# One kernel, several edits: a weight load in two column halves with another front, and a third product buffer with the attention work in three excursions

## The chip, the cores and the metric

The kernel runs on one core of a Trainium2 chip. Its time is the device time of one execution in microseconds; the figure for a kernel is the median of its runs. Beside it there is one profiled execution, whose trace gives every instruction of the five engines (PE for matmuls, with PEld for its weight loads; DVE, ACT and POOL for vector work; SP, which issues transfers) with start and duration, counted from the start of the span.

## The reference

Two branches read the same normalised tokens and are added to the input: local attention with dilation, and a gated MLP that mixes over the sequence.

```python
x  = A_x                              # 1 x 2048 x 512
xn = _layernorm(x)
# attention: 32 heads of 16; token s sees s, s-2, ..., s-14
q, k, v = split(xn @ wqkv)
logits  = einsum('bhsd,bhswd->bhsw', q, k[idx]) * 16 ** -0.5   # idx = s - 2w, masked below 0
a       = einsum('bhsw,bhswd->bhsd', softmax(logits), v[idx]) @ wo
# gated MLP: 512 -> 2 x 688
z  = gelu(xn @ w_in)
z1 = z[..., :688]
z2 = _layernorm(z[..., 688:])
g  = einsum('ts,bsf->btf', w_sp, z2) + b_sp[:, None]
b  = (z1 * g) @ w_out
return x + a + b
```

All inputs and the output are bf16.

## The kernel before

Tokens are cut into 16 tiles of 128 (`NT`), features into 4 chunks of 128 (`C`), and the attention work into two halves of 1024 tokens (`hb`). The order on every engine is written out by hand: each engine runs its instructions in the order in which the lines of the kernel issue them, and a wait holds up all that stands behind it on that engine.

**Front.** SP loads x's first four tiles in three transfers, then `w_z2` (the z2 half of `w_in`, 688 columns) in one (L172), then more of x and `wqk`. PE runs matmuls on ones (`spin`, L98) until data comes. A tile is normalised by statistics (`ln_stats`, L183, DVE), a root (`roots`, ACT), a reciprocal (`recip`, DVE) and `ln_apply` (L188, DVE, writes `xn`), and is turned into `xnT`, which has features on the partitions. Tiles 0 to 3 are transposed on PE (`transpose_pe`, L209) and copied out of PSUM by ACT or DVE. Tiles 4 to 15 go in pairs through the loop at L388: DVE does the statistics and starts a Newton iteration for the inverse root (`ln_newton`, L196), POOL runs its eight steps (L203 to L207), DVE applies it, and SP transposes by DMA (`transpose_dma`, L218).

**Middle, up to L477.** PE computes z2 tiles (`z2_part`, L227: 8 matmuls of 344 columns a tile, then a Gelu on ACT that also sums the row into `zsum`), q and k (`qk_pair` and `qk_chunk`: 8 matmuls of 512 columns, then a cast on ACT into `qk`) and v (`v_pair`, L280). ACT squares each z2 tile for its second moment (`z2_square`, L237); `z2_stats` and `z2_norm` turn sums into mean and inverse root and normalise all 16 tiles on DVE.

For the attention logits DVE multiplies q by shifted k (`products(hb, p)`, L298: two of the eight window positions at a time, 128 x 8192 elements, into a buffer `pr` of a pool of two), and PE sums over the 16 elements of each head with 0/1 weights (`reduce_heads(hb, p)`, L305: 16 matmuls with a 32-column stationary operand). `softmax_top`, `softmax_exp` and `softmax_norm` follow on DVE and ACT. `reduce_heads` and `v_pair` fill PE with matmuls that use 32 of its columns at a time (`tile_position`); the kernel goes into such work and back several times between L438 and L476. Where `prp` has no free buffer, `products` waits on DVE until PE has read one.

**End, from L482.** Sixteen times `mix(j)` (32 matmuls on z2, L492) and `z1_tile(j)`, then the gate; between them DVE works through the attention average (`av_ops`); after the last tile PE computes both output projections (L639, L648) and DVE adds x.

Of the kernel before, what the change touches and what calls it, by code (L numbers as in the profile page):

```python
# [18 lines left out]
H = 32  # L19
DH = 16  # L20
DHA = 14
W = 8
DIL = 2
HALO = 16
# [21 lines left out]
def kernel(  # L46
# [38 lines left out]
    def bank_pair(name, two=False):  # L85
        turn[0] += 1
        pool = ps_b if turn[0] % 3 == 0 and not two else ps_a
        return pool.tile([P, 2, 512], F32, name=name, tag="mm")

    b16 = const.tile([NT, P], BF16, name="b16")  # L90
    A.dma_start(b16[:], B_b_sp.rearrange("(j p) -> j p", p=P))


    ones = const.tile([P, P], BF16, name="ones")
    V.memset(ones[:], 1.0)
# [2 lines left out]
    def spin(n):  # L98
        for _ in range(n):
            PE.matmul(idle[:, 0, 0:P], ones[:], ones[:], start=True, stop=True)  # L100

    spin(26)

    ident = const.tile([P, P], BF16, name="ident")
    G.memset(ident[:], 0.0)
# [4 lines left out]
    for c in range(C):  # L110
# [6 lines left out]
    G.affine_select(out=mask[:], in_=mask[:], compare_op=ALU.is_ge, fill=NEG,  # L117
                    base=-DIL * (W - 1), pattern=[[DIL, W], [1, HALO]], channel_multiplier=0)
    b_col = const.tile([P, NT], F32, name="b_col")
    stats = const.tile([P, NT, 6], F32, name="stats")  # L120
    mv = const.tile([P, NT, 2], F32, name="mv")
    rstd = const.tile([P, NT], F32, name="rstd")
# [3 lines left out]
    V.memset(eps_t[:], EPS)  # L126
    zsum = const.tile([P, NT], F32, name="zsum")
    zsq = const.tile([P, NT], F32, name="zsq")
    zmean = const.tile([P, NT], F32, name="zmean")
    zvar = const.tile([P, NT], F32, name="zvar")  # L130
    zrstd = const.tile([P, NT], F32, name="zrstd")

    z2 = base.tile([P, NT, FH], BF16, name="z2")
# [14 lines left out]

    early = ExitStack()
    e1 = early.enter_context(tc.tile_pool(name="e1", bufs=1))  # L150
    xqp = early.enter_context(tc.tile_pool(name="xqp", bufs=3))
    xnp = early.enter_context(tc.tile_pool(name="xnp", bufs=6))
    w_z2 = e1.tile([P, C, FH], BF16, name="w_z2")
    wqk = e1.tile([P, C, 2, D], BF16, name="wqk")
    junk = e1.tile([P, FH], BF16, name="junk")


    w_in_r = B_w_in.rearrange("(k p) f -> p k f", p=P)
# [9 lines left out]
    x0 = xqp.tile([P, 4, D], BF16, name="xq")  # L168
    SP.dma_start(x0[:, 0, :], x2[0:P, :])  # L169
    SP.dma_start(x0[:, 1, :], x2[P:2 * P, :])  # L170
    SP.dma_start(x0[:, 2:4, :], x2[2 * P:4 * P, :].rearrange("(i p) d -> p i d", p=P))  # L171
    SP.dma_start(w_z2[:], w_in_r[:, :, FH:F])  # L172
    xq.append(x0)
    load_x(1)
    for s in range(2):
# [7 lines left out]
    def ln_stats(i):  # L183
        xs = xq[i // 4][:, i % 4, :]
        V.bn_stats(stats[:, i, :], xs)
        V.bn_aggr(mv[:, i, :], stats[:, i, :])

    def ln_apply(i):  # L188
        xn = xnp.tile([P, D], BF16, name="xn")
        V.tensor_scalar(xn[:], xq[i // 4][:, i % 4, :], mv[:, i, 0:1], rstd[:, i:i + 1], ALU.subtract, ALU.mult)  # L190
        return xn

    def roots(a, b):
        A.activation(rstd[:, a:b], mv[:, a:b, 1], ACT.Sqrt, bias=eps_t[:])

    def ln_newton(a, b):  # L196

        sl = slice(a, b)
        y, h, t = rstd[:, sl], hv[:, sl], nt[:, sl]
        V.tensor_scalar(h, mv[:, sl, 1], EPS, -0.5 / NEWTON_K, ALU.add, ALU.mult)  # L200
        V.tensor_scalar(t.bitcast(I32), h.bitcast(I32), 1, 0x3FFFFFFF, ALU.logical_shift_right, ALU.bitwise_and)
        V.tensor_scalar(y.bitcast(I32), t.bitcast(I32), -1, SEED, ALU.mult, ALU.add)
        for c in NEWTON_C:  # L203
            G.tensor_tensor(t, y, y, ALU.mult)
            G.tensor_tensor(t, t, h, ALU.mult)
            G.tensor_scalar(t, t, c, None, ALU.add)
            G.tensor_tensor(y, y, t, ALU.mult)  # L207

    def transpose_pe(i, xn):  # L209
        pt = ps_aux.tile([P, C, P], BF16, name="pt", tag="aux")  # L210
        for c in range(C):
            PE.transpose(pt[:, c, :], xn[:, c * P:(c + 1) * P], ident[:])  # L212
        if i < 2:
            A.copy(xnT[:, :, i * P:(i + 1) * P], pt[:])
        else:
            V.tensor_copy(xnT[:, :, i * P:(i + 1) * P], pt[:])

# [3 lines left out]
    def z2_start(i):  # L221
        pz = bank_pair("pzb")
        for kc in range(C):
            z2_part(i, pz, kc)
        return pz

    def z2_part(i, pz, kc):  # L227
        for hh in range(2):
            PE.matmul(pz[:, hh, 0:FHALF], xnT[:, kc, i * P:(i + 1) * P],  # L229
                      w_z2[:, kc, hh * FHALF:(hh + 1) * FHALF],  # L230
                      start=(kc == 0), stop=(kc == C - 1))

    def z2_gelu(i, pz):
        A.activation(z2[:, i, :].rearrange("p (a b) -> p a b", a=2), pz[:, :, 0:FHALF],  # L234
                     ACT.Gelu_apprx_tanh, accum_out=zsum[:, i:i + 1])

    def z2_square(i):  # L237
        A.activation(junk[:], z2[:, i, :], ACT.Square, accum_out=zsq[:, i:i + 1])  # L238

    def z2_tile(i):  # L240
        z2_gelu(i, z2_start(i))

    def z2_stats():
        V.tensor_scalar(zmean[:], zsum[:], 1.0 / FH, None, ALU.mult)
        V.tensor_tensor(zvar[:], zmean[:], zmean[:], ALU.mult)
        V.scalar_tensor_tensor(zvar[:], zsq[:], 1.0 / FH, zvar[:], ALU.mult, ALU.subtract)
        A.activation(zrstd[:], zvar[:], ACT.Sqrt, bias=eps_t[:])

    def z2_norm():
        V.reciprocal(zrstd[:], zrstd[:])  # L250
        for i in range(NT):
            V.tensor_scalar(z2[:, i, :], z2[:, i, :], zmean[:, i:i + 1], zrstd[:, i:i + 1],
                            ALU.subtract, ALU.mult)

    def qk_chunk(b, c):
        tsl = slice(b * 512, (b + 1) * 512)
        pq = bank_pair("pq")
        for s in range(2):
            for kc in range(C):
                PE.matmul(pq[:, s, :], wqk[:, kc, s, c * P:(c + 1) * P], xnT[:, kc, tsl],  # L260
                          start=(kc == 0), stop=(kc == C - 1))
        at = HALO + b % 2 * 512
        A.copy(qk[b // 2][:, :, c, at:at + 512], pq[:])  # L263
# [32 lines left out]
    prs = {}  # L296

    def products(hb, p):  # L298
        pr = prp.tile([P, 2, C, SB], BF16, name="pr")
        off = HALO - DIL * (W - 1 - 2 * p)  # L300
        V.tensor_tensor(pr[:], qk[hb][:, 0, :, HALO:HALO + SB].unsqueeze(1).broadcast_to([P, 2, C, SB]),  # L301
                        shifted(qk[hb][:, 1, :, off:off + SB]), ALU.mult)
        prs[hb, p] = pr
# [43 lines left out]
    def recip(i):  # L347
        V.reciprocal(rstd[:, i:i + 1], rstd[:, i:i + 1])

    pb = ps_aux.tile([P, NT], BF16, name="pb", tag="aux")  # L350
    PE.transpose(pb[:], b16[:], ident[0:NT, 0:NT])
    spin(9)
    ln_stats(0)
    roots(0, 1)
    A.copy(b_col[:], pb[:])
    ln_stats(1)
    roots(1, 2)
    recip(0)
    transpose_pe(0, ln_apply(0))
    recip(1)  # L360
    spin(4)
    transpose_pe(1, ln_apply(1))
    spin(4)
    ln_stats(2)
    roots(2, 3)
    ln_stats(3)
    roots(3, 4)
    pz0 = z2_start(0)
    z2_gelu(0, pz0)
    recip(2)  # L370
    xn2 = ln_apply(2)
    recip(3)
    xn3 = ln_apply(3)
    pz1 = bank_pair("pzb")
    for kc in range(2):
        z2_part(1, pz1, kc)
    transpose_pe(2, xn2)
    for kc in range(2, C):
        z2_part(1, pz1, kc)
    transpose_pe(3, xn3)  # L380
    z2_gelu(1, pz1)
    z2_tile(2)
    z2_tile(3)


# [2 lines left out]
    for g in groups + (None,):  # L388
        if g:
            for i in range(*g):  # L390
                ln_stats(i)
            ln_newton(*g)
        if prev:
            for i in range(*prev):
                transpose_dma(i, ln_apply(i))
            if prev[0] == 6:
                SP.dma_start(wv[:], wqkv_r[:, :, 2 * D:3 * D])
        prev = g


# [14 lines left out]
    qk_chunk(1, 2)  # L415
    z2_square(5)
    qk_chunk(1, 3)
    for j in range(5):
        load_wsp(j)
        if j == 1:  # L420
            SP.dma_start(w_z1[:], w_in_r[:, :, 0:FH])


    V.tensor_copy(qk[1][:, 1, :, 0:HALO], qk[0][:, 1, :, SB:SB + HALO])
    products(0, 0)
    products(0, 1)
    z2_square(6)
    z2_tile(7)
    qk_chunk(2, 0)
    qk_chunk(2, 1)  # L430
    z2_square(7)
    qk_chunk(2, 2)
    qk_chunk(2, 3)
    z2_tile(8)
    qk_chunk(3, 0)
    z2_square(8)
    qk_chunk(3, 1)
    reduce_heads(0, 0)  # L438
    reduce_heads(0, 1)
    products(0, 2)  # L440
    products(0, 3)
    v_pair(0)
    v_pair(1)
    qk_chunk(3, 2)
    z2_tile(9)
    qk_chunk(3, 3)
    z2_square(9)
    z2_tile(10)
    z2_square(10)
    z2_tile(11)  # L450
    reduce_heads(0, 2)
    reduce_heads(0, 3)
    products(1, 0)
    v_pair(2)
    products(1, 1)
    softmax_top(0)
    z2_square(11)
    v_pair(3)
    z2_tile(12)
    z2_square(12)  # L460
    z2_tile(13)
    z2_square(13)
    z2_tile(14)
    z2_square(14)
    z2_tile(15)
    z2_square(15)
    v_pair(4)
    z2_stats()
    z2_norm()
    v_pair(5)  # L470
    reduce_heads(1, 0)
    reduce_heads(1, 1)
    products(1, 2)
    softmax_exp(0)
# [231 lines left out]
```

## Time and profile before

| | |
|---|---|
| median of 3 runs | 206.74 us (206.56 to 206.85) |
| the profiled execution | 206.28 us, span 204.6 us |
| PE busy | 199.7 us, granted clock 1.0 |
| DVE, ACT, POOL busy | 165.9, 93.6, 16.1 us |
| first z2 matmul, first q/k matmul, first mix | 6.73, 11.84, 73.16 us |
| matmuls of L492, L260 + L272, L229, L285, L310 (whole span) | 512, 128, 128, 256, 128 |

In a view of the timeline a row gives the start and the duration in us, the engine, the line, the operation, output and inputs with their shapes, how many instructions are merged in the row, and in brackets the idle time ahead of them and what ended it. In the chain of work a row gives start, duration and what the end of the program depended on at that time. "PEclk" on the page is the granted TensorE clock in tenths.

### The profile page before, as it was taken

What the parts mean: (1) busy time and instruction counts of PE and PEld (TensorE: products, weight loads), DVE (VectorE), ACT (ScalarE), POOL (GpSimd) and SP (SyncE); (2) the same over time, 40 slices, a digit from 0 to 9 for tenths busy, and PEclk for the clock granted to TensorE, in tenths of its full rate; (3) what the DMA queues carried; (4) which work ended last, traced back from release to release, by engine and by line L of the source; (5) the groups of instructions that cost most, each with busy time, mean ns of one, the idle gap of its engine ahead of it and who ended that gap; (6) DMA issues with size and microseconds to landing.
All of it is one profiled execution on the core that took longest, in us unless ns stands there. A gap on an engine that the chain in (4) does not pass through costs nothing.

```text
span 204.6 us, 4062 instructions
## 1 busy us (share of the span) xinstructions
PE 199.7 (98%) x1666; PEld 120.1 (59%) x1666; DVE 165.9 (81%) x192; ACT 93.6 (46%) x145; POOL 16.1 (8%) x82
## 2 busy tenths in 40 slices
PE   7999999999999999999999999999999999999994
PEld 6655544555566666656666666666666664444442
DVE  4799949659299499989999999999999988335263
ACT  3868897676879996335733331223333311000000
POOL 5045640000000000100000000000000000000000
PEclk9999999999999999999999999999999999999999
DMA  6974957999000004707857799999756225015633
GB/s 167 365 225 79 187 107 153 187 215 145 0 3 0 3 0 41 170 20 161 125 119 153 176 201 187 196 165 205 141 144 141 56 48 80 10 41 153 240 109 96
DMA packets 67395, 25.64 MB, mean 125 GB/s; under 512 B 57152, under 2 KB 67248, under 8 KB 67248
## 3 DMA queue, kind: packets, MB, share of 16 engines
q1 hardware_dynamic: 66960, 25.24, 58.2%
q8 instruction: 13, 0.21, 0.5%
q10 hardware_dynamic: 416, 0.14, 0.3%
q14 instruction: 6, 0.05, 0.1%
HBM read 9.79 MB, written 2.10 MB: 58 GB/s over the span
## 4 chain that ended last, share of the span: by engine, by line
PE 95%; DMA 2%; SPq 1%; DVE 0%; issue 0%
PE pg L492 37%; PE pq L260 10%; PE po L639 10%; PE pzb L229 9%; PE pz L504 9%; PE pv L285 7%; PE po L648 6%; PE pl L310 4%; PE pq L272 3%; DMA w_z<-in_B_w_in_dram 2%; PE po L621 1%; PE pt L212 0%; SPq L171 0%; DVE ot L623 0%; SPq L170 0%; SPq L169 0%
## 5 line engine op out<-in xcount | busy, mean ns | idle before, releaser
L492 PE MATMUL pg<-z,wspT 128*128 128x344 bf16 x512 | 77.3, 309 | 0.0
L492 PEld LDWEIGHTS <-wspT 128*128 128x128 bf16 x512 | 50.0, 98 | 24.9 <-issue 0.4
L301 DVE TENSOR_TENSOR pr<-qk 128x8192 bf16<-128x8192 bf16 x8 | 35.0, 4424 | 7.4 <-PE pl L310 7.4
L495 ACT ACTIVATE gs<-pg,b_col 128x688 bf16<-128x688 f32 x16 | 13.4, 835 | 52.8 <-PE pg L492 52.8
L558 DVE TENSOR_TENSOR pw<-vp,a_sb 128x4096 bf16<-128x4096 bf16 x16 | 36.2, 2286 | 0.0
L260 PE MATMUL pq<-xnT,wqk 128*128 128x512 bf16 x96 | 21.5, 379 | 0.0
L504 PE MATMUL pz<-w_z,xnT 128*128 128x344 bf16 x128 | 21.3, 309 | 0.0
L229 PE MATMUL pzb<-w_z,xnT 128*128 128x344 bf16 x128 | 20.1, 309 | 0.3 <-DMA w_z<-in_B_w_in_dram 0.3
L639 PE MATMUL po<-wout,uT 128*128 128x512 bf16 x90 | 19.8, 379 | 0.0
L563 DVE TENSOR_TENSOR pw<-pw 128x4096 bf16<-128x4096 bf16 x8 | 18.3, 2289 | 0.1
L655 DVE TENSOR_TENSOR ot<-po,xr 128x512 bf16<-128x512 f32 x15 | 9.7, 687 | 9.4 <-PE po L648 6.9
L229 PEld LDWEIGHTS <-xnT 128*128 128x128 bf16 x128 | 12.3, 98 | 7.2 <-issue 0.7
L504 PEld LDWEIGHTS <-xnT 128*128 128x128 bf16 x128 | 12.4, 98 | 6.5 <-issue 0.4
L260 PEld LDWEIGHTS <-wqk 128*128 128x128 bf16 x96 | 9.3, 98 | 10.9 <-issue 0.4
L639 PEld LDWEIGHTS <-uT 128*128 128x128 bf16 x90 | 8.7, 98 | 10.7 <-issue 0.4
L263 ACT CAST qk<-pq 128x1024 bf16<-128x1024 f32 x12 | 12.2, 1013 | 5.4 <-PE pq L260 5.4
L285 PE MATMUL pv<-xnT,wv 128*32 128x512 bf16 x256 | 14.6, 380 | 0.0
L509 ACT ACTIVATE z<-pz 128x688 bf16<-128x688 f32 x16 | 11.9, 745 | 5.6 <-PE pz L504 5.2
L238 ACT ACTIVATE junk<-z 128x688 bf16<-128x688 bf16 x16 | 12.5, 779 | 0.2
L234 ACT ACTIVATE z<-pzb 128x688 bf16<-128x688 f32 x16 | 11.8, 737 | 1.4 <-PE pzb L229 1.4
L648 PE MATMUL po<-wo_r,op 32*128 32x512 bf16 x224 | 12.3, 374 | 0.0
L285 PEld LDWEIGHTS <-wv 128*32 128x32 bf16 x256 | 9.4, 139 | 4.6 <-issue 0.3
(81 smaller groups left out, 167.5 us busy)
## 6 DMA issues: line engine op xcount, KB each, us to landing
xr<-in_A_x_dram SPq DMA_DIRECT2D x4, 512.0 KB, 4.2
out_dram<-ot SPq DMA_DIRECT2D x15, 128.0 KB, 1.8
wo_r<-in_A_wo_dram SPq DMA_DIRECT2D x4, 448.0 KB, 5.0
w_z<-in_B_w_in_dram SPq DMA_DIRECT2D x2, 688.0 KB, 4.9
xq<-in_A_x_dram SPq DMA_DIRECT2D x2, 512.0 KB, 7.0
wqk<-in_A_wqkv_dram SPq DMA_DIRECT2D x2, 512.0 KB, 7.1
wout<-in_B_w_out_dram SPq DMA_DIRECT2D x1, 640.0 KB, 5.0
a_sb<-in_A_x_dram SPq DMA_DIRECT2D x1, 512.0 KB, 9.2
```

What stands on the lines that cost most here:

```text
L229: PE.matmul(pz[:, hh, 0:FHALF], xnT[:, kc, i * P:(i + 1) * P], w_z2[:, kc, hh * FHALF:(hh + 1) * FHALF], start=(kc == 0), stop=(kc == C - 1))
L238: A.activation(junk[:], z2[:, i, :], ACT.Square, accum_out=zsq[:, i:i + 1])
L260: PE.matmul(pq[:, s, :], wqk[:, kc, s, c * P:(c + 1) * P], xnT[:, kc, tsl], start=(kc == 0), stop=(kc == C - 1))
L285: PE.matmul(pv[32 * k:32 * k + 32, dd, :].rearrange("p (b t) -> p b t", b=NB), wv_v[:, kc, 2 * d2 + dd, :], xnT_g[:, kc, :, k, :], start=( ...
L301: V.tensor_tensor(pr[:], qk[hb][:, 0, :, HALO:HALO + SB].unsqueeze(1).broadcast_to([P, 2, C, SB]), shifted(qk[hb][:, 1, :, off:off + SB]), ...
L492: PE.matmul(pg[:, hh, 0:FHALF], wsps[j][:, k, :], z2[:, k, hh * FHALF:(hh + 1) * FHALF], start=(k == 0), stop=(k == NT - 1))
L495: A.activation(gs[:], pg[:, :, 0:FHALF], ACT.Identity, bias=b_col[:, j:j + 1])
L504: PE.matmul(pz[:, hh, 0:FHALF], xnT[:, kc, j * P:(j + 1) * P], w_z1[:, kc, hh * FHALF:(hh + 1) * FHALF], start=(kc == 0), stop=(kc == C - 1))
L558: V.tensor_tensor(pw[:], shifted(vp[:, :, hb, off:off + P]), a_sb[:, 2 * p:2 * p + 2, osl].unsqueeze(2).broadcast_to([P, 2, DH, P]), ALU.mult)
L563: V.tensor_tensor(pws[p - 1][:], pws[p - 1][:], pw[:], ALU.add)
L639: PE.matmul(pos[jj, k][:], uT[:, m, i * P:(i + 1) * P], wout[:, m, :], start=first and m == 0, stop=not first and m == MCH - 1)
L648: PE.matmul(pos[jj, k][:], op[32 * k:32 * k + 32, d, jj * P:(jj + 1) * P], wo_r[32 * k:32 * k + 32, d, :], start=first and d == 0, stop=(n ...
```

## The change

Front: `w_z2` is loaded in two halves of 344 columns, the first ahead of x's tiles 2 and 3. The load of `b_sp` at the start and its transpose on PE go; later a DMA transpose and a POOL copy make `b_col`. Tile 1's statistics are made by ACT with two accumulating activations, ahead of and behind the root of tile 0. Evacuations of tiles 0 and 1 are split in two. The z2 matmuls of tiles 0 and 1 are issued by column half. In the loop over pairs `ln_newton(*g)` is issued behind the applies and transposes of the pair before, and runs tile by tile with two-operation steps.

Middle: a third product buffer `prx`, placed where `xq` and `xn` lay, serves every third product; three products and three reductions follow one another; the z2 tiles 9 to 15 stand together; tiles 7, 8, 13, 14 and 15 (`ZV`) get mean and variance from DVE's `bn_stats` instead of sums from ACT.

```diff
+ZV = (7, 8, 13, 14, 15)
-    A.dma_start(b16[:], B_b_sp.rearrange("(j p) -> j p", p=P))
-    spin(26)
+    spin(35)
...
     SP.dma_start(x0[:, 1, :], x2[P:2 * P, :])
+    SP.dma_start(w_z2[:, :, 0:FHALF], w_in_r[:, :, FH:FH + FHALF])
     SP.dma_start(x0[:, 2:4, :], x2[2 * P:4 * P, :].rearrange("(i p) d -> p i d", p=P))
-    SP.dma_start(w_z2[:], w_in_r[:, :, FH:F])
+    SP.dma_start(w_z2[:, :, FHALF:FH], w_in_r[:, :, FH + FHALF:F])
...
     def ln_newton(a, b):
...
-        for c in NEWTON_C:
-            G.tensor_tensor(t, y, y, ALU.mult)
-            G.tensor_tensor(t, t, h, ALU.mult)
-            G.tensor_scalar(t, t, c, None, ALU.add)
-            G.tensor_tensor(y, y, t, ALU.mult)
+        for i in range(a, b):
+            y, h, t = rstd[:, i:i + 1], hv[:, i:i + 1], nt[:, i:i + 1]
+            for c in NEWTON_C:
+                G.tensor_scalar(t, y, y, h, ALU.mult, ALU.mult)
+                G.tensor_scalar(y, t, c, y, ALU.add, ALU.mult)
...
         if i < 2:
-            A.copy(xnT[:, :, i * P:(i + 1) * P], pt[:])
+            for c in range(0, C, 2):
+                A.copy(xnT[:, c:c + 2, i * P:(i + 1) * P], pt[:, c:c + 2, :])
...
+    def z2_half(i, pz, hh):
+        for kc in range(C):
+            z2_part(i, pz, kc, (hh,))
...
+    def z2_moments(i):
+        for hh in range(2):
+            V.bn_stats(zst[:, i, hh, :], z2[:, i, hh * FHALF:(hh + 1) * FHALF])
+        V.bn_aggr(zmv[:, i, :], zst[:, i, :, :])
...
     def products(hb, p):
-        pr = prp.tile([P, 2, C, SB], BF16, name="pr")
+        pr = (prx if (4 * hb + p) % 3 == 2 else prp).tile([P, 2, C, SB], BF16, name="pr")
...
-    pb = ps_aux.tile([P, NT], BF16, name="pb", tag="aux")
-    PE.transpose(pb[:], b16[:], ident[0:NT, 0:NT])
-    spin(9)
+    A.activation(zrstd[:, 0:1], eps_t[:], ACT.Sqrt)
     ln_stats(0)
+    A.activation(junk[:, 0:D], x0[:, 1, :], ACT.Identity, scale=-1.0 / D, accum_out=mv[:, 1, 0:1])
     roots(0, 1)
-    A.copy(b_col[:], pb[:])
-    ln_stats(1)
-    roots(1, 2)
+    A.activation(junk[:, 0:D], x0[:, 1, :], ACT.Square, bias=mv[:, 1, 0:1], accum_out=mv[:, 1, 1:2])
+    A.activation(rstd[:, 1:2], mv[:, 1, 1:2], ACT.Sqrt, bias=eps_t[:], scale=1.0 / D)
     recip(0)
     transpose_pe(0, ln_apply(0))
+    spin(7)
     recip(1)
-    spin(4)
-    transpose_pe(1, ln_apply(1))
-    spin(4)
+    xn1 = xnp.tile([P, D], BF16, name="xn")
+    V.tensor_scalar(xn1[:], x0[:, 1, :], mv[:, 1, 0:1], rstd[:, 1:2], ALU.add, ALU.mult)
+    transpose_pe(1, xn1)
...
-    pz0 = z2_start(0)
+    pz0 = bank_pair("pzb")
+    pz1 = bank_pair("pzb")
+    z2_half(0, pz0, 0)
+    z2_half(1, pz1, 0)
+    z2_half(0, pz0, 1)
     z2_gelu(0, pz0)
     recip(2)
     xn2 = ln_apply(2)
     recip(3)
+    transpose_pe(2, xn2)
+    z2_half(1, pz1, 1)
+    z2_gelu(1, pz1)
     xn3 = ln_apply(3)
-    pz1 = bank_pair("pzb")
-    for kc in range(2):
-        z2_part(1, pz1, kc)
-    transpose_pe(2, xn2)
-    for kc in range(2, C):
-        z2_part(1, pz1, kc)
+    pz2 = bank_pair("pzb")
+    z2_part(2, pz2, 0)
+    z2_part(2, pz2, 1)
+    V.bn_stats(stats4[:, 0, :], xq[1][:, 0, 0:D // 2])
     transpose_pe(3, xn3)
-    z2_gelu(1, pz1)
-    z2_tile(2)
+    V.bn_stats(stats4[:, 1, :], xq[1][:, 0, D // 2:D])
+    V.bn_aggr(mv[:, 4, :], stats4[:])
+    z2_part(2, pz2, 2)
+    z2_part(2, pz2, 3)
+    z2_gelu(2, pz2)
     z2_tile(3)
...
         if g:
             for i in range(*g):
-                ln_stats(i)
-            ln_newton(*g)
+                if i > 4:
+                    ln_stats(i)
         if prev:
             for i in range(*prev):
                 transpose_dma(i, ln_apply(i))
...
+        if g:
+            ln_newton(*g)
         prev = g
...
+    SP.dma_start_transpose(b_t[:], B_b_sp.rearrange("(j p) -> j p", p=P))
+    G.tensor_copy(b_col[:], b_t[:])
```

The order of the middle, before and after, one word per call (`q` a q/k chunk, `z` a z2 tile, `R` a reduction, `V` a `v_pair`, `P` a product on DVE), from the products' start to the first mix:

```
before: P00 P01 z7 q20 q21 q22 q23 z8 q30 q31 R00 R01 P02 P03 V0 V1 q32 z9 q33 z10 z11
        R02 R03 P10 V2 P11 softmax_top V3 z12 z13 z14 z15 V4 z2_stats z2_norm V5 R10 R11 P12 V6 V7
after:  P00 P01 P02 z7 q20 q21 q22 q23 z8 q30 q31 q32 R00 R01 R02 P03 moments(7, 8) V0 V1 q33 P10
        z9 z10 z11 z12 z13 z14 z15 P11 moments(13, 14, 15) z2_stats V2 V3 R03 z2_roots softmax_top
        z2_norm V4 R10 V5 R11 P12 V6 V7
```

More of the change, by code (lines that the diff above doesn't have):

```diff
@@ L88, in bank_pair @@
         return pool.tile([P, 2, 512], F32, name=name, tag="mm")
-    b16 = const.tile([NT, P], BF16, name="b16")
-    A.dma_start(b16[:], B_b_sp.rearrange("(j p) -> j p", p=P))
     ones = const.tile([P, P], BF16, name="ones")
@@ L119 @@
     b_col = const.tile([P, NT], F32, name="b_col")
+    b_t = const.tile([P, NT], BF16, name="b_t")
+    stats4 = const.tile([P, 2, 6], F32, name="stats4")
     stats = const.tile([P, NT, 6], F32, name="stats")
@@ L128 @@
     zsq = const.tile([P, NT], F32, name="zsq")
-    zmean = const.tile([P, NT], F32, name="zmean")
-    zvar = const.tile([P, NT], F32, name="zvar")
+    zmv = const.tile([P, NT, 2], F32, name="zmv")
+    zmean = zmv[:, :, 0]
+    zvar = zmv[:, :, 1]
     zrstd = const.tile([P, NT], F32, name="zrstd")
@@ L150 @@
     e1 = early.enter_context(tc.tile_pool(name="e1", bufs=1))
-    xqp = early.enter_context(tc.tile_pool(name="xqp", bufs=3))
-    xnp = early.enter_context(tc.tile_pool(name="xnp", bufs=6))
     w_z2 = e1.tile([P, C, FH], BF16, name="w_z2")
@@ L155 @@
     junk = e1.tile([P, FH], BF16, name="junk")
+    zst = e1.tile([P, NT, 2, 6], F32, name="zst")
+    toks = ExitStack()
+    xqp = toks.enter_context(tc.tile_pool(name="xqp", bufs=3))
+    xnp = toks.enter_context(tc.tile_pool(name="xnp", bufs=6))
     w_in_r = B_w_in.rearrange("(k p) f -> p k f", p=P)
@@ L225, in z2_start, with z2_part @@
         return pz
-    def z2_part(i, pz, kc):
-        for hh in range(2):
+    def z2_half(i, pz, hh):
+        for kc in range(C):
+            z2_part(i, pz, kc, (hh,))
+    def z2_part(i, pz, kc, halves=(0, 1)):
+        for hh in halves:
             PE.matmul(pz[:, hh, 0:FHALF], xnT[:, kc, i * P:(i + 1) * P],
@@ L233, in z2_gelu @@
     def z2_gelu(i, pz):
+        kw = dict(accum_out=zsum[:, i:i + 1]) if i not in ZV else {}
         A.activation(z2[:, i, :].rearrange("p (a b) -> p a b", a=2), pz[:, :, 0:FHALF],
-                     ACT.Gelu_apprx_tanh, accum_out=zsum[:, i:i + 1])
+                     ACT.Gelu_apprx_tanh, **kw)
     def z2_square(i):
@@ L241, in z2_tile, with z2_roots @@
         z2_gelu(i, z2_start(i))
+    def z2_moments(i):
+        for hh in range(2):
+            V.bn_stats(zst[:, i, hh, :], z2[:, i, hh * FHALF:(hh + 1) * FHALF])
+        V.bn_aggr(zmv[:, i, :], zst[:, i, :, :])
     def z2_stats():
[L244 to L247, printed above, removed]
+        for a, b in ((0, 7), (9, 13)):
+            zm, zv = zmean[:, a:b], zvar[:, a:b]
+            V.tensor_scalar(zm, zsum[:, a:b], 1.0 / FH, None, ALU.mult)
+            V.tensor_tensor(zv, zm, zm, ALU.mult)
+            V.scalar_tensor_tensor(zv, zsq[:, a:b], 1.0 / FH, zv, ALU.mult, ALU.subtract)
+    def z2_roots():
+        A.activation(zrstd[:], zvar, ACT.Sqrt, bias=eps_t[:])
     def z2_norm():
@@ L251, in z2_norm @@
         for i in range(NT):
-            V.tensor_scalar(z2[:, i, :], z2[:, i, :], zmean[:, i:i + 1], zrstd[:, i:i + 1],
+            V.tensor_scalar(z2[:, i, :], z2[:, i, :], zmv[:, i, 0:1], zrstd[:, i:i + 1],
                             ALU.subtract, ALU.mult)
@@ L421 @@
             SP.dma_start(w_z1[:], w_in_r[:, :, 0:FH])
+    toks.close()
+    prx = early.enter_context(tc.tile_pool(name="prx", bufs=1, reuse_waits="tile"))
     V.tensor_copy(qk[1][:, 1, :, 0:HALO], qk[0][:, 1, :, SB:SB + HALO])
@@ L426 @@
     products(0, 1)
+    products(0, 2)
     z2_square(6)
@@ L430 @@
     qk_chunk(2, 1)
-    z2_square(7)
     qk_chunk(2, 2)
@@ L435 @@
     qk_chunk(3, 0)
-    z2_square(8)
     qk_chunk(3, 1)
+    qk_chunk(3, 2)
     reduce_heads(0, 0)
     reduce_heads(0, 1)
-    products(0, 2)
+    reduce_heads(0, 2)
     products(0, 3)
+    z2_moments(7)
+    z2_moments(8)
     v_pair(0)
     v_pair(1)
-    qk_chunk(3, 2)
+    qk_chunk(3, 3)
+    products(1, 0)
     z2_tile(9)
-    qk_chunk(3, 3)
     z2_square(9)
     z2_tile(10)
+    z2_tile(11)
     z2_square(10)
-    z2_tile(11)
-    reduce_heads(0, 2)
+    z2_tile(12)
+    z2_tile(13)
+    z2_tile(14)
+    z2_tile(15)
+    z2_square(11)
+    z2_square(12)
+    products(1, 1)
+    for i in (13, 14, 15):
+        z2_moments(i)
+    z2_stats()
+    v_pair(2)
+    v_pair(3)
     reduce_heads(0, 3)
-    products(1, 0)
-    v_pair(2)
-    products(1, 1)
+    z2_roots()
     softmax_top(0)
[L457 to L466, printed above, removed]
+    z2_norm()
     v_pair(4)
-    z2_stats()
-    z2_norm()
+    reduce_heads(1, 0)
     v_pair(5)
-    reduce_heads(1, 0)
     reduce_heads(1, 1)
```

## The prediction

> **What bounds the kernel now.** I read the page first, then the chain of work that ended last, then the timeline of the first 32 us, then DVE and POOL around the products. The page and the chain:
>
> ```profile
> span 204.6 us, 4062 instructions
> PE 199.7 (98%) x1666; PEld 120.1 (59%) x1666; DVE 165.9 (81%) x192; ACT 93.6 (46%) x145; POOL 16.1 (8%) x82
> ...
> 2.19 4.50 DMA w_z<-in_B_w_in_dram
> 6.69 0.04 issue
> 6.73 1.91 PE pzb L229 x12
> ```
>
> TensorE is busy 98% of the span, and the chain is one unbroken row of PE work from 6.73 us to 201.66. Before it stands one transfer, `w_z2`, landing at 6.69. So a gain can only come from three places: PE's real work starting earlier, PE paying less where it changes the kind of its matmuls, and nothing else; and any wait that PE gains is paid in full. The profiled run took 206.28 us, 1.68 around its span; the median of the runs shown is 206.74, so I work in differences and add them to 206.74. A difference under 0.2%, 0.41 us, counts as no change.
>
> The second thing to read is how normalised tokens reach the products, because the change reorders it:
>
> ```profile
> 25.44 0.18 DVE L186 BATCH_NORM_AGGREGATE mv<-stats 128x2 f32<-128x6 f32 x1
> 25.66 0.17 DVE L200 TENSOR_SCALAR hv<-mv 128x2 f32<-128x2 f32 x1
> ...
> 26.15 0.73 DVE L190 TENSOR_SCALAR xn<-a_sb,mv,rstd 128x512 bf16<-128x512 bf16 x2
> ...
> 28.68 0.73 DVE L190 TENSOR_SCALAR xn<-a_sb,mv,rstd 128x512 bf16<-128x512 bf16 x2 [1.79 <-POOL rstd L207]
> 30.40 0.18 DVE L424 COPY qk<-qk 128x64 bf16<-128x64 bf16 x1 [0.99 <-ACT qk L263]
> 30.49 8.75 DVE L301 TENSOR_TENSOR pr<-qk 128x8192 bf16<-128x8192 bf16 x2
> 43.04 8.76 DVE L301 TENSOR_TENSOR pr<-qk 128x8192 bf16<-128x8192 bf16 x2 [3.79 <-PE pl L310]
> ```
>
> ```profile
> 26.31 0.30 POOL L204 TENSOR_TENSOR nt<-rstd 128x2 f32<-128x2 f32 x1 [0.54 <-DVE rstd L202]
> 26.69 0.24 POOL L205 TENSOR_TENSOR nt<-nt,hv 128x2 f32<-128x2 f32 x1
> 27.02 0.21 POOL L206 TENSOR_SCALAR nt<-nt 128x2 f32<-128x2 f32 x1
> 27.32 0.20 POOL L207 TENSOR_TENSOR rstd<-rstd,nt 128x2 f32<-128x2 f32 x1
> ```
>
> POOL's Newton chain of a pair of tiles is eight dependent operations, 0.27 to 0.38 us from one to the next, 2.2 to 2.3 in all. Now each chain runs beside the next pair's statistics and DVE sets the pace, a pair every 2.87 us (L190 at 14.66, 17.53, 20.39, 23.27). The first products end at 39.2; PE uses them at 41.94, so DVE has slack there and even waits 3.79 for its buffer.
>
> **The front, part by part.** The `b16` load, its transpose and nine spins go; they end at 4.75, before PE has data, so they are worth nothing. Splitting `w_z2`: x0's second tile lands at 3.5, x0's other two at 4.6, `w_z2` at 6.69, then 512 KB every 1.5 us (8.3, 9.85, 11.4), so the queue moves some 340 KB a us whatever the size of the transfer. A half (344 KB) takes 1.0: the first lands at about 4.6, x0's tiles 2 and 3 at 5.4 to 5.7, the second half at 6.7 to 7.2. PE then no longer waits for weights, but for `xn1`, since tile 1's transposes stand ahead of all z2 matmuls in its queue.
>
> The Trainium skill ("DMA: Bandwidth & Descriptors", section "Bandwidth") speaks against splitting: batch to 1 MiB or more, with 341 GB/s there and 138 at 64 KB. An estimate of 200 GB/s for a half by that page would put the second half near 8.2, some 0.5 late; the trace, with 512 KB following one another at 340, doesn't show such a loss.
>
> Tile 1's statistics move to ACT. A Square of 688 columns lets the next instruction start 0.82 later (L238); at 512 it is 0.14 less (1024 columns take 1.01, 512 take 0.60). Identity 3.53 to 4.20, root of tile 0 at 4.20 to 4.50, Square to 5.22 with its bias (0.09 more, L495 against L509), root of tile 1 to 5.55, reciprocal, `xn1` at 5.78 to 6.19. On DVE it is ready at 5.74 now: this move makes it 0.45 later. Transposes at 6.25, 0.22 on PE, first z2 matmul at **6.47, 0.26 earlier** than 6.73. From there the same 32 matmuls (0.146 each) and eight transposes (0.055) need 5.11 before the first q/k matmul; now they run without a gap (6.73 + 5.11 = 11.84, as L272 shows). In the new order gaps arise: `xnT` of tile 1 comes in two copies, the second ready at 7.36 for a use at 7.34 (0.05); `xn2` follows `xn1` on DVE (two statistics, reciprocal, apply: 8.32) and PE is free at 8.27 (0.1); transposes 2 and 3 are each covered by four matmuls, 0.58 + 0.22 = 0.80, where transpose, evacuation and wake-up take 0.40 + 0.42 + 0.10 (0.12 twice). That is 0.39 lost, **front +0.1 us**, between -0.25 (no gap) and +0.5.
>
> That ACT runs Square and Identity between two roots without a table load isn't in the trace; copies behind a root (L214), Squares and Identities among Gelus (L238, L495) cost none, so I take zero; a switch costs 1.30 (68.50 to 69.80 at L247), four would cost 5.2.
> The skill ("ScalarE: Activation LUTs", "Table sets: the hidden batching unit") puts copy and identity into every set and doesn't name Square; with the 2.66 that the page gives for a switch ("What ACT_TABLE_LOAD costs"), two switches would be 5.3, while the row says 2.6.
>
> **Attention excursions.** Leaving 128-column matmuls for 32-column ones and back costs PE 0.09 to 0.11 at each border (41.85 to 41.94, 47.13 to 47.24, 54.20 to 54.30, 59.48 to 59.59, 64.26 to 64.36, 73.05 to 73.16), and 0.06 at 67.8 from pv to pl: 0.67 ahead of the first mix. The new order has one excursion less there, four borders and up to three of the small ones: 0.41 to 0.59. I take **-0.15**.
>
> **Newton after the apply.** The new loop issues a pair's Newton start only behind the previous pair's applies, so DVE's applies wait for a chain that no longer runs beside them. The pace becomes: three DVE steps and hand-over 0.66, chain, 0.04, and 0.32 until the next start. The operations stay eight a pair, but all are TENSOR_SCALAR, tile by tile, with per-partition scalars. POOL shows none such. From below: today's chain, 2.23. From above: DVE's TENSOR_SCALAR with two such scalars starts from about 0.27 (410 ns at 512, 459 at 688), with constants it takes 0.17; 0.05 per scalar on twelve gives 0.6 more, 3.1. Nearest is POOL's own TENSOR_SCALAR, 0.30 to the next operation: 2.40, and 0.1 where an apply runs beside it (L204 0.30 against 0.195). I take 2.50, a pair every 3.52 us.
>
> The first Newton start slips from 11.78 to 12.15, since DVE evacuates tile 3 at 10.29 to 10.71, and stats4's second half and aggregate and tile 5's statistics follow. The sixth starts at 12.15 + 5 x 3.52 = 29.75, the last apply at 32.95, the halo copy at 33.27, products at 33.36. Three of 4.38 end at **46.50**. PE: third-block q/k starts at 38.40 + 0.1, three chunks 5.18, border 0.09, two reductions 1.73: it wants the third product at **45.5**. It waits **1.05 us**. Behind it in PE's queue stands everything, so the end moves by it. The SP queue doesn't decide: its transposes (1.3 each) still land before use, the tightest, tile 7, at 21.85 for a use near 22.3.
>
> **What is hidden.** Five Squares leave ACT (46% busy). Five `z2_moments` add some 1.05 each to DVE (from L185's 0.69 at 512): two before products(1,0), which wait for q/k chunk (3,3) at about 52.5 anyway; three ahead of z2_norm. That ends near 75.0 + the stall, against 76.4 now; mix(0), from 72.7, needs its last tile at 77.1 on the same scale: 2.1 of cover. The b_t transpose (1.2 on SP) and its copy on POOL precede 40 us of slack before L495. Late on, DVE ends at 175.8 and its first PE reader of that quarter comes 10 us later. Nothing here costs.
>
> Sum: +0.1 - 0.15 + 1.05 = +1.0; 206.74 + 1.0 = **207.7 us**.
>
> **Rivals.** *Chain long* (per-partition scalars cost POOL what they cost DVE): 3.1, 0.6 x 6 = 3.6 more, 211.3; against it, POOL's two-tensor operations are no dearer than its constant ones. *Hidden anyway*: below a chain of 2.33 the third product is in time, and front and borders cancel: 206.7. Today's chain of 2.23 speaks for it; slack would then be 0.6. *The other side, faster*: the first z2 matmul, freed of the 4.5 us load, starts at 6.47 and `xn2` and the copies keep up: -0.25, borders -0.26: 206.2. It decides from a chain under 2.33 and gaps under 0.1 in all; no more can be had, since PE has no other idle time. *It doesn't do what it says* (a table load in the front, or the second half late): 208 to 209.
>
> **Chances.** Forecast, a stall of 0.5 to 3 us, 0.40; chain long 0.10; front spoiled 0.03; hidden 0.27; faster 0.20. So slower 0.53, same 0.27, faster 0.20. The range drops a tenth on either side: 206.2, within the faster case, to 209.8, within the long one.
>
> **What would show it.** Front: first pzb matmul at 6.4 to 6.6, first L272 matmul at 11.7 to 12.2. Chain: eight POOL operations in 2.4 to 2.6, a pair every 3.5 us, first products near 33.4. Stall: PE idle at the reduction line, released by DVE pr, 1 us, at some 45.5. Borders: q/k 2,3 to mix with 0.1 to 0.25 less in gaps. I am wrong if first products start by 32.2, if PE idles at mix(0) for z2, or if the q/k work starts before 11.5.

## The result and the profile after

The changed kernel takes **211.32 us** (median of 6 runs, 210.7 to 212.71) against 206.59 for the kernel before (6 runs in the same series): a ratio of 1.0238, 95% interval 1.0213 to 1.0263. It is slower by 4.7 us, where 1.0 was forecast. The profiled execution took 210.72, with a span of 208.8; the sums below are of this execution and that of the kernel before (206.28), which differ by 4.4. The page of the changed kernel:

```profile
span 208.8 us, 4072 instructions
PE 200.3 (96%) x1664; PEld 119.8 (57%) x1664; DVE 171.0 (82%) x209; ACT 90.9 (44%) x136; POOL 21.8 (10%) x83
...
PE 76%; DVE 8%; POOL 7%; issue 5%; DMA 2%; SPq 1%
```

PE does the same work and is busy for nearly the same time, but 96% of the span; the third line, the shares of the chain that ended last, had 95% PE before. DVE and POOL, which had next to nothing of it, now hold 15%. The timeline of POOL in the changed kernel shows a whole Newton chain of a pair, tile by tile (L210 and L211 take the place of L204 to L207), and the start of the next one:

```profile
17.02 0.34 POOL L210 TENSOR_SCALAR nt<-rstd,hv 128x1 f32<-128x1 f32 x1 [1.03 <-DVE rstd L206]
17.46 0.27 POOL L211 TENSOR_SCALAR rstd<-nt,rstd 128x1 f32<-128x1 f32 x1
17.83 0.34 POOL L210 TENSOR_SCALAR nt<-rstd,hv 128x1 f32<-128x1 f32 x1
18.27 0.27 POOL L211 TENSOR_SCALAR rstd<-nt,rstd 128x1 f32<-128x1 f32 x1
18.51 0.34 POOL L210 TENSOR_SCALAR nt<-rstd,hv 128x1 f32<-128x1 f32 x1
18.95 0.27 POOL L211 TENSOR_SCALAR rstd<-nt,rstd 128x1 f32<-128x1 f32 x1
19.31 0.34 POOL L210 TENSOR_SCALAR nt<-rstd,hv 128x1 f32<-128x1 f32 x1
19.75 0.26 POOL L211 TENSOR_SCALAR rstd<-nt,rstd 128x1 f32<-128x1 f32 x1
21.05 0.34 POOL L210 TENSOR_SCALAR nt<-rstd,hv 128x1 f32<-128x1 f32 x1 [1.03 <-DVE rstd L206]
```

From 17.02 to 20.01 the chain takes 2.99 us, and POOL then idles 1.03 until DVE starts the next pair. A pair comes every 4.03 us, where it came every 2.87. DVE waits for POOL at the end of each, and so the products start at 36.75 instead of 30.49 (DVE's timeline):

```profile
36.34 0.41 DVE L194 TENSOR_SCALAR xn<-a_sb,mv,rstd 128x512 bf16<-128x512 bf16 x1 [1.06 <-POOL rstd L211]
36.67 0.17 DVE L459 COPY qk<-qk 128x64 bf16<-128x64 bf16 x1
36.75 4.42 DVE L321 TENSOR_TENSOR pr<-qk 128x8192 bf16<-128x8192 bf16 x1
```

PE, in its timeline, finishes two reductions and waits for the third product, with all the rest of the kernel behind it in its queue:

```profile
44.75 1.91 PE L330 MATMUL pl<-pr,rsel 128*32 128x512 bf16 x32
49.90 1.05 PE L330 MATMUL pl<-pr,rsel 128*32 128x512 bf16 x16 [3.23 <-DVE pr L321]
50.77 0.60 PE L305 MATMUL pv<-xnT,wv 128*32 128x512 bf16 x8
```

Thirty-two of these matmuls take 1.73 (starts 0.054 apart), so PE was ready at 46.48 and lost 3.42. Further up in the same timeline PE also waits for transposed tiles:

```profile
19.07 3.75 PE L238 MATMUL pzb<-w_z,xnT 128*128 128x344 bf16 x24
22.94 7.08 PE L280 MATMUL pq<-xnT,wqk 128*128 128x512 bf16 x32
29.85 1.33 PE L238 MATMUL pzb<-w_z,xnT 128*128 128x344 bf16 x8
31.41 7.07 PE L280 MATMUL pq<-xnT,wqk 128*128 128x512 bf16 x32 [0.23 <-DMA xnT<-xn]
```

The whole difference up to the first mix, 77.44 against 73.16 = 4.28, adds up from PE's starts: front +0.32 (first q/k matmul 12.16 against 11.84); transposed tiles 4 to 7 late, 3.87 for three z2 tiles instead of 3.50, +0.37; tiles 8 to 11 late, 29.85 to 31.41 where the z2 tile between needs 1.17, +0.39; third product +3.42; borders -0.23. The sum is 4.27. After that point the two kernels run alike (first mix to output projection 95.36 and 95.24).

### The profile page after: what moved, and what is told of

Its sections match the earlier page's. It is cut to its first block, busy times and chain, and to the rows that moved or that the text cites. A ratio compares the mean times of both kernels' runs of the same rounds, so it can differ in the third digit from the quotient of the medians.

```text
span 208.8 us, 4072 instructions
## 1 busy us (share of the span) xinstructions
PE 200.3 (96%) x1664; PEld 119.8 (57%) x1664; DVE 171.0 (82%) x209; ACT 90.9 (44%) x136; POOL 21.8 (10%) x83
## 4 chain that ended last, share of the span: by engine, by line
PE 76%; DVE 8%; POOL 7%; issue 5%; DMA 2%; SPq 1%
PE pg L527 36%; PE po L674 9%; PE pz L539 9%; PE pv L305 7%; PE po L683 6%; PE pzb L238 5%; POOL nt L210 4%; DVE pr L321 3%; POOL rstd L211 3%; PE pl L330 3%; DMA xq<-in_A_x_dram 2%; DVE xn L194 1%; DVE stats L189 1%; PE pq L280 1%; PE po L656 1%
## 5 line engine op out<-in xcount | busy, mean ns | idle before, releaser
L543 POOL MEMSET z<- 128x80 bf16 x16 | 3.1, 198 | 107.8 <-DMA uT<-z 66.5
```

## The experiments

Each run stands beside runs of the kernel before on the same chip, four kernels or two sharing them; ratios are to those, with their 95% intervals. The first four take the change apart: form of the Newton steps, their place, both, and the front.

**e1: the earlier form in the new place.**

```diff
-        for i in range(a, b):
-            y, h, t = rstd[:, i:i + 1], hv[:, i:i + 1], nt[:, i:i + 1]
-            for c in NEWTON_C:
-                G.tensor_scalar(t, y, y, h, ALU.mult, ALU.mult)
-                G.tensor_scalar(y, t, c, y, ALU.add, ALU.mult)
+        for c in NEWTON_C:
+            G.tensor_tensor(t, y, y, ALU.mult)
+            G.tensor_tensor(t, t, h, ALU.mult)
+            G.tensor_scalar(t, t, c, None, ALU.add)
+            G.tensor_tensor(y, y, t, ALU.mult)
```

> The changed kernel with the Newton steps in their earlier form (four operations for a pair of tiles), still issued behind the applies of the pair before. Theory (the loss is the long POOL chain made serial by the order, and a stall at the third reduction): the chain is 2.2 to 2.35 us again, a pair every 3.3 us, first products near 32.0 instead of 36.75, third product ready at 45.2, PE wants it at 45.7: no stall, 206.5 to 207.0 us. Rival A (the order alone loses it): a pair still comes every 3.5 us or more and PE still waits over 1 us for DVE, 208 or more. Rival B (the new order of the middle loses it, whatever the Newton part does): over 209.

Measured: 207.47 us, ratio 1.0055 (1.0042 to 1.0069). Most of the loss is gone, but not all; the expectation was too low. The chain is 2.2 again (12.87 to 15.05), yet a pair comes every 3.51 us and not 3.3: since both tiles of a pair end together, both applies wait for the whole chain, and 0.65 passes until the next start where the prediction's formula has 0.32. PE in this run:

```profile
44.21 1.91 PE L330 MATMUL pl<-pr,rsel 128*32 128x512 bf16 x32
46.51 1.05 PE L330 MATMUL pl<-pr,rsel 128*32 128x512 bf16 x16 [0.39 <-DVE pr L321]
```

The wait at the same place is 0.57 (46.51 - 44.21 - 1.73), against 3.42. So the order alone has a price, 0.9 us over e3 below. Of Rival A the pace came (3.51), but not its wait of over 1 us nor its 208; Rival B, over 209, falls.

**e2: the new form in the earlier place.**

```diff
                 if i > 4:
                     ln_stats(i)
+            ln_newton(*g)
         if prev:
...
-        if g:
-            ln_newton(*g)
```

> The changed kernel with the Newton start of a pair issued ahead of the applies of the pair before, as it was, and the new form of the steps (scalar operands, tile by tile). Theory: the chain stays 3.0 us but runs beside DVE again, a pair every 3.05 to 3.15 us, first products near 32.0, no stall, 206.5 to 207.1 us; form and place cost much only together. Rival A (the form alone loses it, whatever the place): first products at 34 or later and a stall over 1 us, 208 or more. Rival B (the new middle): over 209.

Measured: 207.20 us, 1.0037 (1.0025 to 1.0049). The chain is as long as in the changed kernel, but POOL runs one chain straight into the next (13.22, 16.23, 19.36, 22.49), a pair every 3.0 to 3.13 us, first products at 32.21, and no wait at the reductions:

```profile
44.48 2.79 PE L330 MATMUL pl<-pr,rsel 128*32 128x512 bf16 x48
47.08 0.40 PE L305 MATMUL pv<-xnT,wv 128*32 128x512 bf16 x4
```

Of the 0.6 over e3, the trace shows 0.25 at the z2 tiles 4 to 6 (3.75 from the first to the next q/k matmul instead of 3.50) and 0.13 in the front; the rest is within the spread of the runs. The median is 0.1 above the range expected.

**e3: both as they were**, the two edits above together.

> The changed kernel with both the earlier form and the earlier place of the Newton steps; front and middle as changed. Theory: all of the stall gone, first products near 31; what is left is the front (+0.3, first q/k matmul at 12.16 against 11.84) and the borders of the excursions (-0.23): 206.6 to 206.8, level with the kernel before. Rival B (the new middle costs by itself): over 207.5.

Measured: 206.61 us, 1.0008 (0.9999 to 1.0017). The loss is gone with the Newton steps alone, and the new middle isn't what costs. DVE, then PE:

```profile
30.91 13.09 DVE L321 TENSOR_TENSOR pr<-qk 128x8192 bf16<-128x8192 bf16 x3
44.08 2.79 PE L330 MATMUL pl<-pr,rsel 128*32 128x512 bf16 x48
```

The third product is done at 44.0 and wanted at 45.8 (44.08 + 1.73): 1.8 us of slack. That explains why one edit alone costs under 1 us and both 4.7. The third product ends at 46.5 in e1, 45.3 in e2 and 49.8 in the changed kernel: 2.5 and 1.3 us later for one edit, 5.8 for both. In the earlier place a longer chain costs only what exceeds DVE's own pace of 2.87 a pair; in the new place all of its length counts, six times over. Of the delay PE pays what exceeds the slack, and 0.25 to 0.76 at transposed tiles.

**e5: the middle alone**, e3 with the front of the kernel before.

```diff
-    SP.dma_start(w_z2[:, :, 0:FHALF], w_in_r[:, :, FH:FH + FHALF])
     SP.dma_start(x0[:, 2:4, :], x2[2 * P:4 * P, :].rearrange("(i p) d -> p i d", p=P))
-    SP.dma_start(w_z2[:, :, FHALF:FH], w_in_r[:, :, FH + FHALF:F])
+    SP.dma_start(w_z2[:], w_in_r[:, :, FH:F])
...
-    A.activation(junk[:, 0:D], x0[:, 1, :], ACT.Identity, scale=-1.0 / D, accum_out=mv[:, 1, 0:1])
...
+    ln_stats(1)
+    roots(1, 2)
...
-    z2_half(0, pz0, 0)
-    z2_half(1, pz1, 0)
-    z2_half(0, pz0, 1)
+    pz0 = z2_start(0)
```

> As the run before it, and the front too as it was (w_z2 in one transfer, tile 1's statistics on DVE, whole copies; the bias still comes by the later transpose): what is left is the third product buffer, the three excursions, the moments on DVE. Theory: PE has three borders of 0.1 us less ahead of the first mix, -0.23 us: 206.3 to 206.45, and 0.3 below the run with the new front. Rival B (the middle costs): over 207. Rival C (the front as changed is neutral): no difference to the run before it.

Measured: median 206.23 us against 206.38, ratio 1.0004 (0.9981 to 1.0027; one of its eleven runs took 208.79): no difference that the times can tell, from the kernel before or, with overlapping intervals, from e3. So Rival B falls, and Rival C isn't excluded. The traces tell the borders: from first q/k matmul to first mix 73.02 - 11.91 = 61.11, against 61.32 before, 0.21 less. e3 needs the same 61.11 (73.37 - 12.26). So the new middle saves 0.2 us of PE time, and in e3 the new front gives it back: 12.26 against 11.91 here. What the front costs is less sure, since its executions scatter: the first q/k matmul comes at 12.06 to 12.39 in five with the new front, at 11.84 to 12.15 in three with the earlier one (e4 has 12.15).

**e4: the Newton edits alone, on the kernel before** (form and place as in the change).

> The kernel before with only the Newton steps changed, form and place together. Theory: a pair every 4.05 us, first products at 36.1 to 36.8 instead of 30.5; this order needs only two products at the first reductions, so PE waits at the second of them, for 1.3 to 2 us, and 0.7 for transposed tiles ahead of it: 208.3 to 209.2 us, about half of the 4.7 lost with the new middle, which asks for three products 2.6 us later. Rival (the Newton steps lose the same everywhere): 210.5 or more. Rival (they are hidden without the new middle): 206.4.

Measured: 208.80 us, 1.0112 (1.0088 to 1.0135), as expected. First products at 36.57; PE, after one reduction, waits for the second product:

```profile
42.87 1.05 PE L310 MATMUL pl<-pr,rsel 128*32 128x512 bf16 x16
45.37 1.05 PE L310 MATMUL pl<-pr,rsel 128*32 128x512 bf16 x16 [1.46 <-DVE pr L301]
```

1.64 here, 0.6 at the transposed tiles. The same Newton steps cost 2.3 in this middle and 4.7 in the new one (with its front), which asks DVE for three products of 4.4 us by 45.8 (e3) where the old one asks for two by 42.8 (the kernel before, 41.94 + 0.86).

**e9: the suspected cost made larger.** The first operation of each Newton step is issued twice:

```diff
                 G.tensor_scalar(t, y, y, h, ALU.mult, ALU.mult)
+                G.tensor_scalar(t, y, y, h, ALU.mult, ALU.mult)
```

> The changed kernel with one of the two POOL operations of each Newton step issued twice (same result): the suspected cost made larger. Theory: each of six chains grows by four operations of 0.37 to 0.44 us, 1.5 to 1.8, a pair every 5.6 to 5.8 us, and all of it is paid at the end: 9 to 10.6 us more, 220 to 222 us. Rival (the chain is partly hidden, the stall has another cause): under 216.

Measured: 222.1 us (two runs), 10.8 more than the changed kernel. DVE's applies at the chain's end stand 5.79 apart (23.74, 29.53, 35.32, 41.11) instead of 4.04; six times 1.75 is 10.5. Every microsecond of chain is paid at the end: the first mix comes at 88.00 instead of 77.44, 10.56 later. The waits lie in part earlier here, at transposed tiles, and show a second effect. PE, then a window table (start and end; busy time and instructions of PE, PEld, DVE, ACT, POOL; granted clock, DMA share, GB/s):

```profile
45.34 1.33 PE L239 MATMUL pzb<-w_z,xnT 128*128 128x344 bf16 x8
49.89 6.79 PE L281 MATMUL pq<-xnT,wqk 128*128 128x512 bf16 x24 [3.22 <-DMA xnT<-xn]
```

```profile
50.00:54.00 4.00, 4.00 (x13) 1.49 (x12) 4.00 (x2) 0.73 (x1) 0.84 (x1) 0.64 0.69 154
54.00:58.00 4.00, 4.00 (x41) 1.74 (x43) 4.00 (x2) 2.57 (x4) 0.00 (x0) 1.00 1.07 255
```

Behind a wait of 3.22 us the granted clock is 0.64 on average for four microseconds, and 24 matmuls that need 5.18 at full clock take until 56.61, 6.72. These 1.5 us of PE are not paid at the end here, because PE then still waits 1.94 for the third product.
The Trainium skill ("TensorE: Matmul & The Clock Gate", "Part 1: The HAM clock gate") says that PE drops to half its clock after an idle window of about 3.4 us, returns after about as long of sustained work, and that this window runs freely. The half clock agrees (0.50 from 49.5 to 52.6 in finer windows of the same trace), and so does the time that it lasts, 3.2 us. The length of a single wait doesn't decide here: the changed kernel's wait at the third product, 3.23 us by the same view, kept a clock of 1.0 in its profiled execution, and earlier in e9 the clock is 0.50 from 26.6 to 32 behind waits of only 2.06 and 1.00 us.
Two of the changed kernel's six runs had a mean clock of 0.992 and took 212.4 and 212.7 us, the others 210.7 to 211.7. Nothing shows that a drop behind the third-product wait made them longer: single executions of the kernel before and of e5, which have no such wait, had 0.991 or 0.992 as well.

**e6: w_z2 halved by contraction.** e3 with rows of 1376 bytes kept whole, and the matmuls in that order:

```diff
-    SP.dma_start(w_z2[:, :, 0:FHALF], w_in_r[:, :, FH:FH + FHALF])
+    SP.dma_start(w_z2[:, 0:2, :], w_in_r[:, 0:2, FH:F])
     SP.dma_start(x0[:, 2:4, :], x2[2 * P:4 * P, :].rearrange("(i p) d -> p i d", p=P))
-    SP.dma_start(w_z2[:, :, FHALF:FH], w_in_r[:, :, FH + FHALF:F])
+    SP.dma_start(w_z2[:, 2:4, :], w_in_r[:, 2:4, FH:F])
```

> The changed kernel with the earlier Newton steps (as e3_old_newton), and w_z2 split by halves of the contraction, so that its rows stay 1376 bytes, the z2 matmuls in the matching order. Theory (rows of 688 bytes cost the queue 0.85 us, and x's tiles 2 and 3 wait for that): first half lands at 4.5 to 4.8 instead of 5.3 to 5.5, tiles 2 and 3 at 5.4 instead of 6.0 to 6.3, first q/k matmul 0.2 to 0.3 earlier than in e3: 206.3 to 206.45. Rival (the split itself, two transfers, costs): landings as in e3, 206.6.

Measured: 206.39 us, 0.9989 (0.9976 to 1.0003). The time lies where the theory put it, but not for its reason: the landings (first half 5.6, x 6.3, second half 7.7) are those of the column halves (changed kernel 5.5, 6.3, 7.5; e3 5.3, 6.0, 8.0), as the rival said, and the first q/k matmul comes at 12.19. The row size isn't the cause.

**e7: the parts that helped, put together.** e5 with w_z2 by contraction halves, and the z2 matmuls of tiles 0 and 1 in the order of the halves:

```diff
+    SP.dma_start(w_z2[:, 0:2, :], w_in_r[:, 0:2, FH:F])
     SP.dma_start(x0[:, 2:4, :], x2[2 * P:4 * P, :].rearrange("(i p) d -> p i d", p=P))
-    SP.dma_start(w_z2[:], w_in_r[:, :, FH:F])
+    SP.dma_start(w_z2[:, 2:4, :], w_in_r[:, 2:4, FH:F])
...
-    pz0 = z2_start(0)
+    z2_part(0, pz0, 0)
+    z2_part(0, pz0, 1)
+    z2_part(1, pz1, 0)
+    z2_part(1, pz1, 1)
+    z2_part(0, pz0, 2)
+    z2_part(0, pz0, 3)
```

> The new middle and the earlier Newton steps (as e5_middle_only), w_z2 by contraction halves, tile 1's statistics on DVE, and z2 matmuls of tiles 0 and 1 by halves, so that two and four matmuls or more cover each transposed tile. Theory: first z2 matmul at 6.35 instead of 6.7 to 6.8, no gaps up to the first q/k matmul at 11.45 to 11.6: 205.8 to 205.95, faster than the kernel before by 0.2 to 0.3%. Rival (PE's start isn't bound by w_z2 alone, or gaps eat it as in the changed front): 206.2 or more.

Measured: **205.99 us**, 0.9978 (0.9964 to 0.9991): the one version faster than the kernel before, by 0.5 us between the medians and 0.2% by the ratio. In its profiled execution the middle gives 0.2 of it (first q/k matmul to first mix 61.12), the front next to nothing: the first q/k matmul comes at 11.81, where 11.45 to 11.6 was expected and the kernel before has 11.84:

```profile
6.25 1.34 PE L237 MATMUL pzb<-w_z,xnT 128*128 128x344 bf16 x8 [0.21 <-ACT xnT L218]
7.80 0.74 PE L237 MATMUL pzb<-w_z,xnT 128*128 128x344 bf16 x4 [0.21 <-DMA w_z<-in_B_w_in_dram]
```

z2 starts at 6.25, a little ahead of the 6.35 expected, and then waits for the second half, landed at 7.8.

**e10: w_z2 whole, ahead of x's tiles 2 and 3**, and **e11: x's tiles 2 and 3 ahead of both halves**; the SP orders, on e5 and e7:

```diff
+    SP.dma_start(w_z2[:], w_in_r[:, :, FH:F])
     SP.dma_start(x0[:, 2:4, :], x2[2 * P:4 * P, :].rearrange("(i p) d -> p i d", p=P))
-    SP.dma_start(w_z2[:], w_in_r[:, :, FH:F])
```

```diff
-    SP.dma_start(w_z2[:, 0:2, :], w_in_r[:, 0:2, FH:F])
     SP.dma_start(x0[:, 2:4, :], x2[2 * P:4 * P, :].rearrange("(i p) d -> p i d", p=P))
+    SP.dma_start(w_z2[:, 0:2, :], w_in_r[:, 0:2, FH:F])
```

> As e5_middle_only (new middle, earlier front and Newton steps), with w_z2 whole but issued ahead of x's tiles 2 and 3. It asks what made the halves land late. Theory (two transfers instead of one cost the queue): w_z2 whole lands at 5.5 to 5.7, in the time that its first half took, tiles 2 and 3 at 6.2 to 6.4. Rival (whatever comes third lands late, its size aside): w_z2 lands at 6.5 or later. Time: PE starts z2 at 6.3, but xn2 comes at 8.5 and the transposes of tiles 2 and 3 stand ahead of other work, so the start is lost again: 206.1 to 206.4.

> As e7_mixed_best, with x's tiles 2 and 3 issued ahead of both halves of w_z2 (by contraction). Theory: x's tiles land at 4.6 again, the first half at 5.5 to 6.0, the second at 6.7 to 7.5 where PE wants it at 7.4: first z2 matmul at 6.25 and no wait for xn2 or for weights, first q/k matmul at 11.35 to 11.6 instead of 11.81: 205.7 to 205.9. Rival (two transfers cost, so the first half lands after 6.5): no better than e7, 206.0 or more.

Measured: e10 206.90 us, 1.0017 (1.0001 to 1.0032), slower than expected; w_z2 landed at 6.2 and x at 7.0, between the theory's and the rival's numbers, and PE waited 1.02 for `xn2`. e11 206.47 us, 0.9991 (0.9971 to 1.0011), with runs from 205.68 to 207.38; in its profiled execution x landed at 4.7, the first half at 5.8 and the second only at 8.9, for which PE waited 1.47: the time is the rival's, 206.0 or more, but its late first half did not come. Behind x's second tile, landed at 3.5, the 944 KB of `w_z2` and x's tiles 2 and 3 would all be in at 6.3, an estimate at the 340 KB a us of the later loads. They are in at 6.7 to 7.0 in the earlier order (the kernel before, e4, e5), at 7.0 in e10 and at 7.5 to 8.9 with halves; five executions that share their first five loads (the changed kernel, e1, e2, e3, e9) have 7.5 to 8.1. What delays the last of them stays open; size of rows and order don't settle it.

## Why the prediction was wrong

**The step that failed is the length of the Newton chain,** the 2.50 us in the pace of a pair. The prediction had the direction, the mechanism, the place of the wait and both ends of the price, 2.23 and 3.1 us; it then took 2.50, from POOL's TENSOR_SCALAR with a constant. It measured 2.99 (e1, with the earlier form, has 2.18). The rows fit a price for each per-partition scalar on POOL: 0.27 us with one and a constant (L211), 0.34 with two (L210), 0.07 more, where the prediction read some 0.05 from DVE's rows. L206 before takes 0.21 with a constant, but it does one operation and not two, so how much of the step from 0.21 to 0.27 is the operand's isn't separated. With 2.99 the prediction's own formula, 1.02 + chain, gives a pair every 4.01; measured 4.03 to 4.19.

The rival *chain long* had it at 211.3; the kernel takes 211.32. Its chance should have been the larger, since the only rows that showed the operand at all were DVE's, and a row of the same engine without the operand says nothing of the operand. That its number fits so closely is partly luck: it has a chain of 3.1, a wait of 4.65 and nothing for late transposed tiles, where 2.99, 3.42 and 0.76 were measured.

**The wait at the third product** was put at 45.5 and 1.05 us (46.50 less 45.5 is 1.0); PE was ready at 46.48 and waited 3.42. The third product ended 3.3 us later than forecast (49.8), and PE came 1.0 later, 0.22 by the front and 0.76 by the tiles below. e1, e2, e3 and e9 show cause and slope; e4 shows that the size of the wait depends on the middle, with its front, that asks DVE for the products.

**"The SP queue doesn't decide"** failed with it, a term that the sum had at nothing: at the slower pace the transposed tiles 4 to 11 come late, +0.76 in all, which e3 takes away (3.50 and 1.17 again). So the sum +0.1 - 0.15 + 1.05 became +0.32 - 0.23 + 3.42 + 0.76.

**The front** was right in sign (+0.1 predicted, +0.32 in the profiled execution; first q/k matmul 12.16, within the stated 11.7 to 12.2). The first z2 matmul came at 6.35, 0.38 earlier and not 0.26, but 0.70 went in gaps instead of 0.39. One term was wrong: the halves were to land at 4.6 and 6.7 to 7.2, with x at 5.4 to 5.7; they landed at 5.5 and 7.5, with x at 6.3. "340 KB a us whatever the size" doesn't hold there, and the second half near 8.2, the estimate that the prediction set aside, lies within the 7.5 to 8.9 of the runs. Tile 2's statistics waited for x; `xn2` was ready at 8.51 instead of 8.32, and PE waited for it until 8.57. The gaps at transposes 2 and 3 came as computed, 0.11 each where 0.12 was put. ACT ran Identity and Square between two roots without a table load, as taken.

**The borders** were right: 0.67 to 0.44, -0.23, within the -0.08 to -0.26 stated; 0.21 in e5. **What is hidden** was right too: the moments, the bias and z2_norm (73.1 to 79.4 against a first mix at 77.44, which takes the tiles one after another) cost nothing. (Its mix(0) "from 72.7" is low: 73.16 + 0.1 - 0.15 is 73.1, which only adds cover.)

## What to carry to other kernels

Where two engines hand work to and fro, look at the order in which the first of them issues: a chain that runs beside the next item's work costs nothing until it outlasts it, and the same chain, started only when the last item is done, is paid in full for every item. Two such edits, a longer chain and the later start, cost under 1 us each here and 4.7 together: the later start makes all of the longer chain count, and the slack that hid either is used up. So read the slack at the consumer before pricing either. And price an operand from rows that have that operand, on whatever engine, rather than from the same engine without it.

## What the runs showed of the hardware

- On POOL a TENSOR_SCALAR of two operations on one element a partition takes 0.27 us with one per-partition scalar and 0.34 with two; one of a single operation with a constant, on two elements, takes 0.21, and a TENSOR_TENSOR on two 0.195.
- Two early transfers of 344 KB landed later in sum than one of 688 KB (7.5 to 8.9 against 6.7 to 7.0), with rows of 688 or 1376 bytes alike.
- In e9 a PE wait of 3.22 us was followed by four microseconds at a mean granted clock of 0.64; the changed kernel's wait of 3.23 us was followed by a clock of 1.0.
